# Rows of the attention by batch, input weights fetched by one transfer, the first group solved in 30 steps, a planner that counts instruction blocks

## The chip, the cores and the metric

The kernel runs on one core of one Trainium2 chip. The metric is the device time of one execution in microseconds. A core has five engines with a queue each: TensorE (PE in the profile; PEld is its weight loads), VectorE (DVE), ScalarE (ACT), GpSimd (POOL) and SyncE (SP), which here only issues transfers. A queue runs in the order in which the program was written. The engines wait for each other through semaphores.

## What is computed

A delta-rule attention (4 batches, 8 heads, 768 tokens, head size 48), then two MLPs with hidden size 2048, each with its own weights:

```python
for t in range(S):                                   # attention
    y[:, :, t] = einsum('bhd,bhde->bhe', q[:, :, t], state)
    v_old = einsum('bhde,bhd->bhe', state, kt)       # kt: normalised key
    state = state + bt * einsum('bhd,bhe->bhde', kt, vt - v_old)
...
h = x @ w_in; g = P(h) / (Q(h) + 1e-6); x = g @ w_out   # first MLP, P cubic, Q quadratic in |h|
...
h = x @ w_in; g = h * tanh(softplus(h)); out = g @ w_out # second MLP
```

The inputs are float64 in memory; the weights are 8-byte numbers that the kernel turns into pairs of 4-byte ones.

## The kernel before

**Attention.** The 768 tokens are cut into 24 steps of 32 tokens (`C`), four steps to a group (`GU`), six groups. The four 32-row quarters of the partitions hold eight of the 32 batch-head pairs each. For a group, `norms` normalises the keys, `prepare` transposes keys and queries and multiplies them (`gram`, L407), `inverse` solves a unit triangular system for the whole group, and `finish` transposes the solution (L499) and multiplies it by beta (L504). Then `step` runs four times, one after the other, since each needs the state of the one before: `ks` (L575: keys times state), `rest` (L581: v minus that, on DVE), `uu` (L587: solution times rest), `s_mm` (L601: the new state), `y_mm` (L622: the output, a part from the state and a part from U), `x_mm` (L634, L638: transposes the output into the MLP's layout). For the first step the state is a tile of zeros.

**The solve.** Groups in `HALVED` (0 and 1) solve two 16-row halves side by side, in 14 steps of two instructions each (L468, L474), and join the halves by two products on PE, `right` (L519) and `left` (L526), of 128 small matmuls each, with an ACT and a DVE operation behind. Other groups take 30 steps and no product. Group 0 is solved on DVE, the others on POOL.

**Rows.** Before, the batch-head pairs lie in the partitions such that the head dimension in `x` comes out permuted. That is why the first MLP's `w_in` is fetched in seven transfers for each 128-column slice (L705, L708, L709), why its slabs are read in the order `slab`, and why `x_mm` has two transposes and four small products.

**Weights.** `Weights.plan` converts a slice of 128 columns of `w_in` or rows of `w_out` (a half): fetch into one of five raw buffers, clamp on POOL (L712, one of three work buffers), fold on ACT (L717), shift and tail on DVE (L726, L731), high part on ACT (L738), low part by two matmuls on PE (L746, L747) and an ACT copy (L750), and a store to memory. 24 halves are planned ahead of the first MLP's first unit.

**MLPs.** A group of 512 tokens is a stretch of 16 units per MLP. A unit is `up` (L846, nine matmuls), the elementwise chain on ACT, DVE and POOL, and `down` (L852, nine matmuls). The first stretch is the first MLP on group 0, the second is the second MLP on group 0 with the four steps of group 1 between its units, and so on.

**Order.** `Plan` holds every operation with an engine, a duration the author wrote down, what it reads and writes, and a due time. `order` lists them by a simulated clock: of the operations that are ready on an engine it takes the one that is due earliest, less its `early`. `run` then writes the program in that order, and fills planned gaps of PE ahead of the MLPs with up to six matmuls that nobody reads (`heat`, L994).

## Time and profile before

| | us |
|---|---|
| runs (3): median, lowest, highest | 1161.53, 1159.25, 1161.65 |
| the profiled execution, its own time | 1155.55 |
| span in its trace | 1153.8 |
| busy: PE, PEld | 1061.0, 850.6 |
| busy: DVE, ACT, POOL | 672.4, 604.0, 543.2 |
| first matmul of the first MLP starts | 125.91 |
| first matmul of the second MLP starts, about | 229 |

PE is busy in 92% of the span. Busy time is an average over stretches with different limits: ahead of 125.9 us no MLP work runs, behind 327 us PE is nearly always busy. The granted clock of PE is 0.97 on the mean and lower in parts of the first 130 us.

### The profile page before, as it was taken

Reading aid. Unit: us, or ns where it says so; the run is one execution under the profiler, and the core shown is the slowest. Engines: PE = TensorE matmul, PEld = TensorE weight load, DVE = VectorE, ACT = ScalarE, POOL = GpSimd, SP = SyncE. Lnnn points to the kernel's source line nnn. Section 1 sums busy time; section 2 is a strip of 40 time slices with the busy share of each in tenths; the row PEclk is TensorE's granted clock in tenths of the full one; section 3 lists DMA queues with packets and bytes.
Section 4 is the critical chain, followed back from the end, with each engine's and each line's share of the span. In section 5 each row is a group of like instructions: output and inputs, shape, how many; then the busy total and the mean of one; then the engine's idle time right before and its main releaser. Section 6 shows DMA issues by size and latency. Waiting matters only on the chain.

```text
span 1153.8 us, 34301 instructions
## 1 busy us (share of the span) xinstructions
PE 1061.0 (92%) x14560; PEld 850.6 (74%) x14560; DVE 672.4 (58%) x1017; ACT 604.0 (52%) x1065; POOL 543.2 (47%) x697
## 2 busy tenths in 40 slices
PE   5477898879999989999999998999999999999997
PEld 4355676667777767777877776877777778889997
DVE  6744687786769934239952239952347668831211
ACT  3333786654568742248842248842257568742221
POOL 4101388754537797818628217728226357600000
PEclk8868998989999999999999999999999999999999
DMA  5755752387776746366765366865466456766773
GB/s 151 211 169 196 237 159 70 112 286 249 238 251 158 233 124 184 109 160 162 223 190 172 113 159 162 224 196 166 113 168 172 131 144 189 191 181 188 202 206 82
DMA packets 118200, 202.86 MB, mean 176 GB/s; under 512 B 48128, under 2 KB 61440, under 8 KB 118048
## 3 DMA queue, kind: packets, MB, share of 16 engines
q1 hardware_dynamic: 117072, 199.41, 60.2%
q8 instruction: 114, 1.87, 0.7%
q10 hardware_dynamic: 848, 1.18, 0.4%
q14 instruction: 38, 0.31, 0.1%
q0 software_dynamic: 128, 0.10, 0.0%
HBM read 168.40 MB, written 29.88 MB: 172 GB/s over the span
## 4 chain that ended last, share of the span: by engine, by line
PE 60%; DVE 5%; ACT 5%; POOL 4%; DMA 3%; issue 2%; SPq 1%; DVEq 0%; POOLq 0%; ACTq 0%
PE b_h L846 25%; PE b_o L852 19%; PE b_o L861 4%; PE b_t L622 3%; PE b_t L601 2%; PE b_t L587 1%; PE b_t L861 1%; POOL xs L474 1%; POOL tmp L468 1%; PE b_t L575 1%; DMA wd<-win 1%; DMA arena<-in_q_dram 1%; POOL mq L884 1%; DVE mq L889 1%; DVE b_r L890 1%
## 5 line engine op out<-in xcount | busy, mean ns | idle before, releaser
L846 PE MATMUL b_h<-x,win 128*128 128x512 f32 x1620 | 411.8, 400 | 16.9 <-DVE ms L886 8.1
L846 PEld LDWEIGHTS b_h<-x,win 128*128 128x128 f32 x1620 | 299.6, 189 | 88.6 <-DVE ms L886 14.1
L852 PE MATMUL b_o<-gh,wout 128*128 128x512 f32 x1332 | 336.7, 398 | 7.0 <-POOL gh L893 5.7
L852 PEld LDWEIGHTS b_o<-gh,wout 128*128 128x128 f32 x1332 | 246.0, 189 | 63.4 <-POOL gh L893 10.3
L884 POOL TENSOR_TENSOR mq<-mq,mr 128x512 f32<-128x512 f32 x96 | 124.2, 1294 | 108.2 <-ACT mr L882 104.8
L897 DVE TENSOR_TENSOR gh<-mq,gh 128x512 fp32r<-128x512 f32 x96 | 72.5, 755 | 163.0 <-ACT mq L896 162.8
L895 ACT ACTIVATE gh<-b_h 128x512 fp32r<-128x512 f32 x96 | 57.3, 597 | 205.3 <-PE b_h L846 201.4
L893 POOL TENSOR_TENSOR gh<-mq,gh 128x512 fp32r<-128x512 f32 x96 | 124.1, 1293 | 56.3 <-ACT gh L892 55.4
L885 DVE TENSOR_TENSOR ms<-ms,b_h 128x512 f32<-128x512 f32 x96 | 65.6, 683 | 53.9 <-ACT ms L883 53.2
L712 POOL TENSOR_SCALAR arena<-arena 128x384 f32<-128x384 f32 x64 | 34.8, 546 | 97.9 <-PE b_h L746 55.8
L876 ACT ACTIVATE mr<-mq,cst 128x512 f32<-128x512 f32 x96 | 69.0, 720 | 20.4 <-POOL mq L884 19.5
L878 ACT ACTIVATE mq<-b_h 128x512 f32<-128x512 f32 x96 | 56.8, 591 | 42.9 <-PE b_h L846 37.7
L889 DVE SCALAR_TENSOR_TENSOR mq<-mq,b_r 128x512 f32<-128x512 f32 x96 | 65.1, 679 | 22.7 <-ACT b_r L888 22.3
L883 ACT ACTIVATE ms<-b_h,ab 128x512 f32<-128x512 f32 x96 | 73.8, 770 | 4.1 <-PE b_h L846 3.7
L468 POOL TENSOR_TENSOR tmp<-xs 128x58 f32<-128x58 f32 (+9 forms) x134 | 70.1, 523 | 9.7
L886 DVE SCALAR_TENSOR_TENSOR ms<-ms,ab,b_h 128x512 f32<-128x512 f32 x96 | 71.7, 747 | 2.9
L474 POOL TENSOR_TENSOR xs<-xs,tmp 128x58 f32<-128x58 f32 (+9 forms) x134 | 68.3, 510 | 10.5
L890 DVE SCALAR_TENSOR_TENSOR b_r<-ms,ab,b_r 128x512 f32<-128x512 f32 x96 | 72.0, 750 | 0.0
L892 ACT CAST gh<-mq 128x512 fp32r<-128x512 f32 x96 | 59.0, 614 | 21.9 <-DVE mq L891 20.1
L891 DVE SCALAR_TENSOR_TENSOR mq<-mq,b_r 128x512 f32<-128x512 f32 x96 | 65.8, 686 | 2.8
L888 ACT ACTIVATE b_r<-mr 128x512 f32<-128x512 f32 x96 | 57.7, 601 | 6.5 <-DVE mq L891 5.7
L896 ACT ACTIVATE mq<-b_h 128x512 f32<-128x512 f32 x96 | 56.9, 593 | 0.0
(179 smaller groups left out, 1415.0 us busy)
## 6 DMA issues: line engine op xcount, KB each, us to landing
win<-wd SPq DMA_DIRECT2D x164, 384.0 KB
wout<-wd SPq DMA_DIRECT2D x164, 384.0 KB
arena<-in_moe_w_out_dram SPq DMA_DIRECT2D x32, 384.0 KB
wd<-x SPq DMA_DIRECT2D x24, 384.0 KB
wd<-win SPq DMA_DIRECT2D x16, 384.0 KB
wd<-wout SPq DMA_DIRECT2D x16, 384.0 KB
arena<-in_moe_w_in_dram SPq DMA_DIRECT2D x16, 384.0 KB
arena<-in_moe_w_in_dram SPq DMA_DIRECT2D x32, 96.0 KB
```

The costliest lines, as they stand in the source:

```text
L468: eng.tensor_tensor(out=tv, in0=part(row, slice(j, j + 1), slice(j + 1, L)).to_broadcast([128, nb, j, n]), in1=part(xs, slice(0, j), slice ...
L474: eng.tensor_tensor(out=to, in0=to, in1=tv, op=ALU.add)
L846: nc.tensor.matmul(out=h, lhsT=win[:, a, j], rhs=x[:, c, slab[j]], start=n == 0, stop=n == 8)
L852: nc.tensor.matmul(out=self.banks[f"o{d}"], lhsT=wout[:, a, d], rhs=gh[:, c], start=first and j == 0, stop=last and j == 2,)
L876: act(out=r, in_=q, func=ACTF.Ln, bias=k["c"])
L883: p.add("ACT", 775, lambda: act(out=s, in_=h, func=ACTF.Identity, scale=k["a3"], bias=k["a2"]), [hb], [sb])
L884: p.add("POOL", 1335, lambda: P.tensor_tensor(out=q, in0=q, in1=r, op=ALU.mult), [rb], [qb])
L886: p.add("DVE", 750, lambda: V.scalar_tensor_tensor(out=s, in0=s, scalar=k["a1"], in1=h, op0=ALU.add, op1=ALU.mult), [hb], [sb])
L889: p.add("DVE", 685, lambda: V.scalar_tensor_tensor(out=q, in0=q, scalar=1.0 + 1e-6, in1=rp, op0=ALU.add, op1=ALU.mult), ["r"], [qb])
L890: p.add("DVE", 750, lambda: V.scalar_tensor_tensor(out=rp, in0=s, scalar=k["a0"], in1=rp, op0=ALU.add, op1=ALU.mult), [sb], ["r"])
L893: p.add("POOL", 1320, lambda: P.tensor_tensor(out=gh[:, 1], in0=q, in1=gh[:, 0].bitcast(F32), op=ALU.subtract), [qb], [ghb])
L897: p.add("DVE", 755, lambda: V.tensor_tensor(out=gh[:, 1], in0=q, in1=gh[:, 0].bitcast(F32), op=ALU.subtract), [qb], [ghb])
```

## The change

It does six things.

1. A quarter of the partitions now holds the eight heads of one batch (`batch`), so that `x` comes out in the order of the model dimension. k and q are fetched in two transfers instead of four, v in four instead of two; `w_in` of the first MLP is fetched in one transfer per slice; `slab` goes; `x_mm` is three transposes.
2. Group 0 leaves `HALVED`: its solve takes 30 steps on DVE and no joining products.
3. The first step of all drops its work on the zero state: no `ks`, no `rest`, half of `y_mm`. The state tiles are no longer cleared.
4. `betas`: fetch and transpose of beta are planned operations; they stood in `setup`.
5. The planner gives PE operations a count of instructions (`ins`) and lets PE wait at every 256 of them until `FETCH` ns after the block before; planned transfers are taken first come, first served.
6. Constants: `NEAR` halved; group 0's queries get `early=FIRST`; the operation on `ab` loses its `early`.

```diff
-HALVED = (0, 1)
+HALVED = (1,)
-NEAR = 40000
+NEAR = 20000
+FETCH = 4000
+AHEAD_INS = 384
...
+        word, block, landed = -AHEAD_INS, 0, []
...
+                ins = self.ops[i][7]
+                word += ins
+                while ins and word >= 256:
+                    word -= 256
+                    part = min(word, ins) * self.ops[i][1] // ins
+                    block = max(end - part, block + FETCH)
+                    end = block + part
...
+    @staticmethod
+    def batch(e):
+        return 2 * (e % 2) + 1 - e // 2
...
         def x_mm():
-            for a in range(2):
-                out = x_ps.rearrange("p k (a n) -> p a k n", a=2)[:, a, 0:2]
-                nc.tensor.transpose(out=out, in_=y[:, a * 4 * D:a * 4 * D + 128], identity=self.ident)
-            for a in range(2):
-                for r in range(2):
-                    rows = slice(64 * r, 64 * r + 64)
-                    nc.tensor.matmul(
-                        out=x_ps[rows, 2, 64 * a:64 * a + 64], lhsT=y[rows, a * 4 * D + 128:(a + 1) * 4 * D],
-                        rhs=self.ident[rows, rows], start=True, stop=True,
-                    )
+            for k in range(3):
+                nc.tensor.transpose(out=x_ps[:, k], in_=y[:, k * 128:(k + 1) * 128], identity=self.ident)
...
-        p.add("PE", 780, ks, [kb, f"{sb}0", f"{sb}1"], [bc], early=lead(AHEAD, G))
-        p.add("DVE", 560, rest, [bc, vb], ["r2"], early=lead(AHEAD, G))
-        p.add("PE", 760, uu, ["r2", f"xt{g}"], [bc], early=lead(AHEAD, G))
+        if u:
+            p.add("PE", 780, ks, [kb, f"{sb}0", f"{sb}1"], [bc], early=lead(AHEAD, G), ins=128)
+            p.add("DVE", 560, rest, [bc, vb], ["r2"], early=lead(AHEAD, G))
+        p.add("PE", 760, uu, ["r2" if u else vb, f"xt{g}"], [bc], early=lead(AHEAD, G), ins=128)
...
-            elif self.n:
+            else:
                 nc.sync.dma_start(out=raw, in_=self.w_in.rearrange("(k p) f -> p k f", p=128)[:, :, cols])
-            else:
-                w = self.w_in.rearrange("(m r d) f -> m d r f", r=2, d=48)
...
-        slab = (1, 0, 2) if m == 1 else (0, 1, 2)
```

What it moves shows in the order of the queues. On PE, from the last work ahead of the solve's result to the first step. Before (L519 and L526 are the joining products, L994 the filler, L746 and L747 the low part of a weight half, L407 a `gram` of the queries, L575 `ks`, L587 `uu`):

```order
L994 MATMUL b_o_100<-ident_138 128x128 x6
L519 MATMUL b_t_102<-xt_162,lg_160 32x16 x128
L994 MATMUL b_o_100<-ident_138 128x128 x2
L746 MATMUL b_h_99<-arena,ident_138 128x384
L747 MATMUL b_h_99<-x_112,minus 128x384
L526 MATMUL b_t_102<-xs_161 16x16 x128
...
L407 MATMUL b_t_103<-kq_146 32x32 x32
L575 MATMUL b_t_102<-su_156,kq_145 32x48 x32
...
L587 MATMUL b_t_102<-r_159,xt_162 32x48 x32
```

And now, in the same place (L447 is `gram`, L1016 the filler, L627 `uu`, L641 `s_mm`):

```order
L447 MATMUL b_t_103<-kq_145 32x32 x32
...
L447 MATMUL b_t_103<-kq_146 32x32 x32
...
L447 MATMUL b_t_103<-kq_147 32x32 x32
L1016 MATMUL b_o_100<-ident_138 128x128 x6
L447 MATMUL b_t_103<-kq_148 32x32 x32
L1016 MATMUL b_o_100<-ident_138 128x128 x6
L627 MATMUL b_t_102<-qv_143,xt_162 32x48 x32
L1016 MATMUL b_o_100<-ident_138 128x128 x2
L641 MATMUL b_o<-u_158,kn_142 64x48
```

All four `gram` of group 0's queries now stand ahead of the first `uu`; before, one stood ahead of it and two behind, between the steps. Both joining products and the first `ks` are gone.

On DVE, where the transposition of v (L245, now L279) cuts into the solve. Before:

```order
L468 TENSOR_TENSOR tmp_163<-xs_161,b_o 128x72
L474 TENSOR_TENSOR b_o<-b_o,tmp_163 128x2x3x12
L245 STREAM_TRANSPOSE qv_143<-ev_134 128x48x8x4
L468 TENSOR_TENSOR tmp_163<-xs_161,b_o 128x88
L474 TENSOR_TENSOR b_o<-b_o,tmp_163 128x2x4x11
```

And now (L508 and L514 are the two instructions of a step, L453 the masking of a `gram`):

```order
L508 TENSOR_TENSOR tmp_163<-xs_161,b_o 128x168
L514 TENSOR_TENSOR b_o<-b_o,tmp_163 128x7x24
L453 TENSOR_TENSOR am_151<-b_t_103,mask_140 128x256
L279 STREAM_TRANSPOSE qv_143<-ev_134 128x48x8x4
L508 TENSOR_TENSOR tmp_163<-xs_161,b_o 128x184
```

It stood behind step 3 of 14 and stands behind step 7 of 30. In neither does a weight conversion stand between the solve's first and last step.

On ACT, at the start of the second MLP. Before (L895 and L896 are the second MLP's function, L717 the fold and L738 the high part of a weight half):

```order
L738 CAST wout_120<-arena 128x384
L895 ACT_TABLE_LOAD
L895 ACTIVATE gh_131<-b_h_99 128x512
L717 ACT_TABLE_LOAD
L717 ACTIVATE arena<-arena 128x384 x2
L895 ACT_TABLE_LOAD
L895 ACTIVATE gh_130<-b_h_98 128x512
L896 ACTIVATE mq_122<-b_h_98 128x512
```

And now (L917 and L918 are that function, L762 the high part):

```order
L762 CAST wout_121<-arena 128x384
L917 ACT_TABLE_LOAD
L917 ACTIVATE gh_130<-b_h_98 128x512
L918 ACTIVATE mq_122<-b_h_98 128x512
L917 ACTIVATE gh_131<-b_h_99 128x512
L918 ACTIVATE mq_122<-b_h_99 128x512
```

The two folds stand ahead of the first table load now, and two table loads are gone.

## Rows read from the trace of the kernel before

**Rows 1.** The page: busy time, share of the span and instructions of each engine.

```profile
PE 1061.0 (92%) x14560; PEld 850.6 (74%) x14560; DVE 672.4 (58%) x1017; ACT 604.0 (52%) x1065; POOL 543.2 (47%) x697
```

**Rows 2.** Stretches: length, busy time of PE, PEld, DVE, ACT, POOL, clock, DMA.

```profile
78.20:125.90 47.70, 38.06 (x1423) 29.24 (x1423) 21.33 (x40) 22.42 (x52) 8.00 (x11) 0.89 0.57 185
125.90:229.00 103.10, 90.67 (x1164) 69.77 (x1162) 81.61 (x124) 74.08 (x133) 77.63 (x101) 0.95 0.45 139
229.00:327.00 98.00, 91.09 (x1537) 70.67 (x1538) 72.43 (x121) 53.10 (x107) 49.13 (x60) 0.97 0.79 258
327.00:1154.00 827.00, 798.91 (x9353) 648.07 (x9351) 448.89 (x645) 427.42 (x721) 390.98 (x478) 1.00 0.62 170
```

**Rows 3.** Timeline of PE, 57 to 126 us: start, length, [idle before and releaser].

```profile
57.23 2.47 PE L519 MATMUL b_t<-xt,lg 32*32 32x16 f32 x169 [12.29 <-DVE xt L499]
62.41 1.37 PE L519 MATMUL b_t<-xt,lg 32*32 32x16 f32 x87 [2.71 <-issue]
...
78.18 0.68 PE L587 MATMUL b_t<-r,xt 32*32 32x48 f32 x26
...
125.91 1.32 PE L846 MATMUL b_h<-x,win 128*128 128x512 f32 x5
```

**Rows 4.** DMA queues, 78.2 to 125.9 us: packets, MB, share.

```profile
q8 instruction: 11, 0.18, 1.6%
```

**Rows 5.** Waits, 78.2 to 125.9 us: us in total, times, longest.

```profile
POOL arena L712 <- PE b_h L746: 30.7, 7, 7.0
...
PE b_t L587 <- issue: 4.3, 3, 2.2
...
PE b_o L622 <- issue: 4.0, 3, 2.0
```

**Rows 6.** Timeline of DVE: the solve of group 0 and what follows.

```profile
35.95 2.00 DVE L448 STREAM_TRANSPOSE b_o<-lg 128x1024 f32<-128x1024 f32 x1
...
41.19 0.18 DVE L468 TENSOR_TENSOR tmp<-xs,b_o 128x28 f32<-128x28 f32 x1 [0.22 <-ACT xs L485]
...
41.64 0.21 DVE L468 TENSOR_TENSOR tmp<-xs,b_o 128x52 f32<-128x52 f32 x1
...
46.34 2.80 DVE L245 STREAM_TRANSPOSE qv<-ev 128x1536 f32<-128x1536 f32 x1 [3.70 <-DMA ev<-in_v_dram]
...
50.78 0.27 DVE L468 TENSOR_TENSOR tmp<-xs,b_o 128x112 f32<-128x112 f32 x1
...
51.40 0.27 DVE L468 TENSOR_TENSOR tmp<-xs,b_o 128x112 f32<-128x112 f32 x1
...
55.28 1.89 DVE L499 STREAM_TRANSPOSE xt<-b_o 128x1024 f32<-128x1024 f32 x1
...
72.38 0.42 DVE L504 TENSOR_TENSOR xt<-xt,beta_t 128x256 f32<-128x256 f32 x1
```

**Rows 7.** Timelines of ACT and, last row, PE at the start of the second MLP.

```profile
237.83 1.28 ACT L717 ACT_TABLE_LOAD   x1
239.13 0.94 ACT L717 ACTIVATE arena<-arena 128x384 f32<-128x384 f32 x2
240.08 1.28 ACT L895 ACT_TABLE_LOAD   x1
...
242.51 2.07 PE L846 MATMUL b_h<-x,win 128*128 128x512 f32 x4 [5.33 <-ACT mq L896]
```

**Rows 8.** Timeline of PE: one `x_mm` of group 1, then four transposes of a `prepare`.

```profile
286.66 0.44 PE L634 MATMUL b_t<-ident,y 128*128 128x128 f32 x2
...
287.40 1.43 PE L846 MATMUL b_h<-x,win 128*128 128x512 f32 x5
...
321.07 0.60 PE L395 MATMUL b_t<-ident,kn 128*128 128x128 f32 x4
321.43 2.32 PE L846 MATMUL b_h<-x,win 128*128 128x512 f32 x9
```

**Rows 9.** Groups by line, 57 to 126 us: busy us, mean ns of one.

```profile
L731 DVE SCALAR_TENSOR_TENSOR arena<-arena,b_r 128x384 int32<-128x384 int32 x15 | 8.3, 551 | 0.4
```

More of the change, by code (lines that the diff above doesn't have):

```diff
@@ L85, in order @@
         for i in range(n - 1, -1, -1):
-            engine, ns, fn, need, more, due, early = self.ops[i]
+            engine, ns, fn, need, more, due, early, ins = self.ops[i]
             if due is not None:
@@ L108, in order @@
             queue = ready[engine]
-            pick = min((x for x in queue if x[0] <= t), key=lambda x: (late[x[1]], x[1]))
+            pick = min((x for x in queue if x[0] <= t), key=lambda x: (x[0] if engine == "DMA" else late[x[1]], x[1]))
             queue.remove(pick)
@@ L116, in order @@
                 was = wide
+                ins = self.ops[i][7]
[5 more added lines that the diff above has]
+                    end = block + part
+            if engine == "DMA":
+                landed.append(end + self.LANDING)
             free[engine] = end
@@ L138, in run, with lead @@
                 fn()
-def lead(ns, G):
+FIRST = 20000
+def lead(ns, G, what=""):
+    if G == 0 and what == "q":
+        return FIRST
     return ns if G > 1 else NEAR * G
@@ L547, in finish @@
         for g in range(GU):
-            p.add(engine, 690 if engine == "POOL" else 420, scale(g), (), [f"xt{g}"], early=lead(AHEADX, G))
+            p.add(engine, 690 if engine == "POOL" else 420, scale(g), ["beta"], [f"xt{g}"], early=lead(AHEADX, G))
     def step(self, p, u):
@@ L616, in y_mm @@
         def y_mm():
-            for part in range(2):
+            for part in range(u == 0, 2):
                 for m in range(M):
@@ L624, in y_mm @@
                             rhs=U[rows, m, :] if part else S[rows, c, m, :],
-                            start=not part and m == 0, stop=part > 0 and m == M - 1, skip_group_check=True,
+                            start=part == (u == 0) and m == 0, stop=part > 0 and m == M - 1, skip_group_check=True,
                         )
```

137 lines of the change are left out of this document (70 added, 67 removed).

## The prediction

> **What bounds the kernel now.** The page's busy shares come first: PE 92% [rows 1]. An average hides where the other 8% lie, so the stretches come next [rows 2]. From 327 us to the end PE is busy 798.9 of 827 us: there only PE work counts. From 125.9 to 229 (first MLP, group 0) it is 90.7 of 103.1, from 229 to 327 91.1 of 98. Ahead of 125.9 no MLP runs; the attention's first group, a chain of single operations, decides when the MLPs start. So the questions are: how much earlier does the first MLP matmul (125.91 us, last of [rows 3]) come, is that kept, and what PE work goes in the rest.
>
> In the last part ahead of it, 78.2 to 125.9, PE runs the four steps of group 0, from the first `uu` (78.18) on. It is busy 38.06 of 47.7 us and idle 9.6. The waits name who ends that idle time: "issue", where no engine and no transfer is late, 4.3 us before `uu` and 4.0 before `y_mm` [rows 5], and little else on PE. The same happens inside one loop of like matmuls: L519 stops 2.71 us after 169 of its 256, with nothing to wait for [rows 3]. The DMA rows say what is missing: 11 packets of 16 KB for the instruction queue in 47.7 us [rows 4]. The order of the program has 2,844 PE instructions there (a float32 matmul is two loads and two matmuls in the trace, a transpose one of each), so a packet is 256 instructions, 47.7/11 = 4.3 us apart. Small matmuls use up 256 instructions faster than that. So this part is bound by PE's instruction supply, with PE's own work close behind.
>
> **The change, part by part.** *Start of the solve.* Before, the matrix is turned at 35.95 to 37.95, and the first of the 14 steps starts at 41.19, after an ACT copy [rows 6]. Ahead of it the change takes six of seven issues per `w_in` slice off SP. That is SP time, not path, but ACT and DVE get weights earlier and may reach the copy earlier. Ends: 38.4 (turn plus copy) and 41.2; I take 40.
>
> *The solve itself.* A step's pace: 41.64 − 41.19 = 0.45 us at 28 elements, 51.40 − 50.78 = 0.62 at 112 [rows 6], so 0.45 + 0.0020 per element above 28. The 14 steps have 1,120 elements in all: 6.3 + 1.5 = 7.8 us. The 30 steps have j(31−j), 4,960 in all: 13.5 + 8.3 = 21.8 us. That is 14 us more on DVE, in the path. Elements beyond 112 are not in the trace; a straight line is assumed, since two pieces of it agree with the instruction's length (0.18 at 28, 0.27 at 112).
>
> *In between.* The turn of v takes 2.80, and DVE waited 3.70 for v's transfer [rows 6]; with the solve longer and the transfer issued from a shorter SP queue I take 0.5 of that wait (ends 0 and 3.7). Three maskings stand between the steps now, 0.42 each as the 0.42 us operations of the same size (1.3 in all).
>
> *Behind the solve.* Before: turn of the solution at 55.28, two products with PE starved (2.71 us in the first), and beta at 72.38, so that `uu` started at 78.18 after `ks` and `rest` on zeros. Now: the turn 1.9, beta 0.4, `uu`. Sum: 40 + 21.8 + 2.8 + 0.5 + 1.3 + 1.9 + 0.4 + 0.2 for a hop = 69 us (ends 67 and 74), against 78.2.
>
> *The four steps.* From `uu` to the first `up` the new order has 2,408 instructions: two `gram` less, half a `y_mm` less, four `x_mm` at 6 for 20, two weight halves more. At 4.3 us per 256 that is 40.4 us. But PE pauses during the solve, and after the pause of 12.29 us at 57.23 it ran 169 matmuls with their loads, some 340 instructions, before it starved [rows 3]: 5.7 us' worth lie ready. That leaves 34.7. PE's own work is 38.06 less some 5 for what is gone, plus 2 for the two halves: 35. Two limits this close do not overlap fully, and the pause lowers the clock (0.89 on the mean in this part, [rows 2]). I take 38; ends 35 and, if nothing is gained, 47.7. First `up` at 69 + 38 = 107 instead of 125.9: **−18.9 us** (ends −4 and −24).
>
> *Is it kept?* The stretch behind it is the same work in nearly the same order, and PE is busy 88% of it [rows 2]; I cost the shift of it at nothing. What covers this is that the weight halves keep up. POOL waited 30.7 us for a buffer that PE's low part had to free [rows 5], so the conversion was waiting for PE, not PE for it, and PE gets to it sooner now. DVE has 21.3 us of work in the 47.7 [rows 2]; with two more halves at 2 x 0.55 [rows 9] and the turn of group 1's queries, as long as v's, it is some 26 of the new 38: 70%, no bound.
>
> *Start of the second MLP.* ACT loads its function tables three times, with two folds between; PE stands for 5.33 us behind it [rows 7]. In the new order the folds stand ahead and two loads go: 2 x 1.28 + 0.94 = **−3.5 us** (ends 0, if a fold ahead is late instead, and −5.3).
>
> *`x_mm`.* Its slot on PE before is 287.40 − 286.66 = 0.74 us; four transposes take 321.43 − 321.07 = 0.36 [rows 8]; three take no more. 0.38 for each of the 20 steps of groups 1 to 5, where PE is the bound: **−7.6 us** (−5 if PE waits in some of them anyway).
>
> *At nothing*: beta's planned fetch (POOL is free then), the uncleared state, v's four issues for two (SP has more time than before), `ab` without `early`.
>
> Sum: −18.9 − 3.5 − 7.6 = −30.0. Against the profiled execution's own 1155.55 us that is 1125.5. It is 6.0 below the median of the runs, so I put the median at 1161.5 − 30.0 = **1131.5**. The ends of the parts give −9 to −37: 1152 to 1124.
>
> **A rule against it.** The trace shows PE stopping in the middle of like matmuls for 2.71 us, and packets 4.3 us apart [rows 3, 4]. The Trainium skill (Runtime: NRT & Kernel Launch, Instruction fetch mechanics) says that instructions come in blocks of 256 while the current ones run, and that the cost of crossing a block is mostly hidden. By that rule the idle time would have another cause and stay. The blocks agree with the trace; "mostly hidden" doesn't, where the matmuls are small.
>
> **The rivals.**
> - *The idle time isn't the supply.* The 9.6 us stay, and only PE's own work goes: from `uu` to `up` 35 + 9.6 = 44.6, first `up` at 113.6, −12.3 − 3.5 − 7.6 = −23.4: 1138. For it: only three loops show it plainly. Against: 11 packets fit the 2,844 instructions.
> - *The gain is given back in the second stretch.* Group 1's steps now stand later among its units: its last `x_mm` behind the 32nd `up`, where it was behind the 30th. If group 1's own chain (POOL's solve, v) sets the pace, the first MLP on group 1 starts some 8 us earlier at most. With `x_mm` in groups 2 to 5 (16 x 0.38 = 6.1) that gives −14: 1147. For it: POOL is busy 77.6 of 103 us [rows 2]. Against: PE is busy 91 of 98 in the second stretch and waits for POOL little.
> - *Slower: the conversion becomes the bound.* Between the first and last step of the solve DVE converts no weights, and 13 of 24 halves remain behind it. If they go through one after another, at clamp, fold, shift, tail, high and low part and copy, six operations of some 0.55 us like that in [rows 9] and 1 to 2 for PE, 5 us a half, plus a wait for a fetch into one of five buffers, 6 in all, it is 13 x 6 = 78 us: first `up` at 147, +21 − 11 = +10: 1171. It decides above 5.4 us a half ((139 − 69)/13); before, 11 went through in 47.7 us, 4.3 each, and they waited for PE.
>
> **How the numbers follow.** Forecast 1131.5: 0.63. Idle time stays: 0.14. Given back: 0.15. Slower: 0.05; its turning point, within 0.2% (2.3 us, about what a measurement can tell): 0.03. Faster 0.92. The range takes in the ends of the parts and the second rival: 1121 to 1151.
>
> **What would show it.** In the new trace: the first `uu` near 69 and the first `up` near 107, 9 or 10 instruction packets between them, hardly any "issue" before the first step. The solve's 60 DVE instructions in about 22 us without, and 27 with, v's turn and the maskings. One table load at the start of the second MLP, and no 5 us gap on PE there. `x_mm` as three transposes in a slot below 0.4. The second MLP's start about 20 us earlier than 229, the first MLP on group 1 about 23 earlier than 327. It is wrong if DVE's pace rises above the line beyond 112 elements, if `up` waits for weights, or if the two later starts have moved by less than the first.

## The result and the profile after

The changed kernel takes 1120.1 us (median of four runs, 1118.1 to 1122.2), the kernel before 1160.4 beside it: a ratio of 0.965 (0.963 to 0.968). The forecast of 1131.5 is 11 us above that, and the range ended at 1121. One execution of `more_ins` (1462 us) and one of the kernel before beside it (2564 us) were slow ones and are left out of the medians below. The profiled execution of the changed kernel took 1122.17 us, with a span of 1120.5; before it was 1155.55 and 1153.8. So the profiles lie 33.4 us apart and the medians 40.3.

The page of the kernel after, busy time and instructions of each engine (of before: [rows 1]):

```profile
PE 1044.5 (93%) x13788; PEld 844.6 (75%) x13788; DVE 684.3 (61%) x1045; ACT 601.4 (54%) x1062; POOL 544.2 (49%) x695
```

PE is busy 16.5 us less, so half of the 33 us in the profiles is PE work that is gone and half is idle time. Where they went shows in stretches of the kernel after: from the start to the first `uu`, to the first `up`, the first stretch (16 units), the first four units of the second MLP, on to unit 64, and the rest. Columns as in [rows 2].

```profile
0.00:66.31 66.31, 38.33 (x675) 32.30 (x675) 53.99 (x110) 24.20 (x48) 16.63 (x45) 0.81 0.66 195
66.31:113.10 46.79, 36.91 (x1205) 27.77 (x1205) 28.31 (x47) 24.19 (x56) 8.65 (x12) 0.84 0.66 213
113.10:214.30 101.20, 90.43 (x1162) 70.99 (x1160) 81.53 (x127) 77.77 (x137) 81.86 (x107) 0.93 0.50 161
214.30:231.30 17.00, 14.77 (x65) 11.23 (x55) 16.35 (x25) 11.33 (x24) 13.34 (x15) 0.90 0.89 316
231.30:486.60 255.30, 245.21 (x3889) 194.08 (x3889) 164.03 (x245) 130.58 (x237) 155.66 (x219) 0.99 0.67 193
486.60:1120.50 633.90, 618.82 (x6807) 508.21 (x6805) 340.09 (x494) 333.32 (x564) 268.08 (x299) 1.00 0.62 173
```

The first number behind a stretch is its length, the next PE's busy time. The same stretches of the kernel before, of a second profiled execution of the changed kernel (`same_again`, below) and of the run with part 1 of the change alone (`rows_only`, below), beside the terms of the forecast:

| stretch | before | after | again | part 1 alone | after − before | forecast |
|---|---|---|---|---|---|---|
| to the first `uu` | 78.2 | 66.3 | 67.1 | 70.5 | −11.9 | −9.2 |
| to the first `up` | 47.7 | 46.8 | 44.8 | 47.7 | −0.9 | −9.7 |
| units 0 to 16 | 103.0 | 101.2 | 101.2 | 102.9 | −1.8 | 0 |
| units 16 to 20 | 23.4 | 17.0 | 16.9 | 24.0 | −6.4 | −3.5 |
| units 20 to 64 | 258.5 | 255.3 | 256.0 | 254.9 | −3.2 | −3.0 |
| unit 64 to the end | 643.0 | 633.9 | 634.4 | 635.4 | −9.1 | −4.6 |
| sum | 1153.8 | 1120.5 | 1120.4 | 1135.4 | −33.3 | −30.0 |

(The 7.6 us for 20 `x_mm` are split 8 to 12.) The sum was only 3.3 us off, but its terms were not that near: one was nearly empty, and the others were larger than forecast. That they cancelled is luck.

The largest miss first. PE from the first `uu` on, timeline of the kernel after (start, length, idle before and releaser):

```profile
66.31 1.50 PE L627 MATMUL b_t<-qv,xt 32*32 32x48 f32 x64 [6.01 <-DVE xt L544]
...
82.66 0.53 PE L662 MATMUL b_o<-su,kq 64*32 64x48 f32 x27 [1.97 <-issue]
...
87.89 0.54 PE L615 MATMUL b_t<-su,kq 64*32 64x48 f32 x31 [2.37 <-issue]
...
99.97 0.37 PE L627 MATMUL b_t<-r,xt 32*32 32x48 f32 x14
104.30 1.32 PE L627 MATMUL b_t<-r,xt 32*32 32x48 f32 x50 [3.96 <-issue]
```

The first `uu` came at 66.3, near the 69 forecast. Then PE still stops in the middle of like matmuls, as in [rows 3], once for 3.96 us. The waits of PE from 66.3 to 113.1 (us in total, times, longest) and the instruction queue in the same time (packets, MB, share), which answer to [rows 4, 5]:

```profile
PE b_t L627 <- issue: 4.8, 2, 4.0
PE b_o L662 <- issue: 2.7, 2, 2.0
PE b_t L615 <- issue: 2.4, 1, 2.4
```

```profile
q8 instruction: 9, 0.15, 1.3%
```

There are 9 packets, as forecast, but 5.2 us apart where 11 packets lay 4.3 apart before. PE is busy 36.9 us (forecast: 35) and idle 9.9, as long as before (9.6); three other executions of this prologue (below) have 35.2 to 38.5 busy and 6.6 to 9.4 idle.

What PE stands for shows when its instructions in the trace are counted, loads and matmuls. The first stop of over 0.25 us comes after 625 of them, at 75.4 us, and the later ones 255 or 510 after the one before (a few records are missing). At each, PE goes on 1.3 to 1.6 us after a 16 KB packet of the instruction queue has landed. Cut into such blocks of 256, the stretch has eight whole ones: three with much work of PE's own (4.45, 5.79 and 4.93 us) and no stop behind them, and five with less (2.85 to 4.40 us) and stops of 0.7 to 4.0 us.

The solve of group 0 on DVE, which answers to [rows 6]:

```profile
35.68 1.98 DVE L488 STREAM_TRANSPOSE b_o<-lg 128x1024 f32<-128x1024 f32 x1
...
42.95 2.93 DVE L279 STREAM_TRANSPOSE qv<-ev 128x1536 f32<-128x1536 f32 x1
...
51.62 0.41 DVE L508 TENSOR_TENSOR tmp<-xs,b_o 128x240 f32<-128x240 f32 x1
...
52.51 0.40 DVE L508 TENSOR_TENSOR tmp<-xs,b_o 128x240 f32<-128x240 f32 x1
...
63.91 1.89 DVE L539 STREAM_TRANSPOSE xt<-b_o 128x1024 f32<-128x1024 f32 x1
65.83 0.43 DVE L544 TENSOR_TENSOR xt<-xt,beta_t 128x256 f32<-128x256 f32 x1
```

A step of 240 elements takes 52.51 − 51.62 = 0.89 us; the straight line of the forecast gives 0.45 + 0.0020 x 212 = 0.87. The turn of v has no wait in front.

The start of the second MLP on ACT, which answers to [rows 7], has one table load, and PE (last row, its own timeline) waited 2.1 us for the `mq` that starts at 220.82, instead of 5.33:

```profile
219.03 1.28 ACT L917 ACT_TABLE_LOAD   x1
220.32 0.60 ACT L917 ACTIVATE gh<-b_h 128x512 fp32r<-128x512 f32 x1
220.82 0.59 ACT L918 ACTIVATE mq<-b_h 128x512 f32<-128x512 f32 x1
...
221.46 3.91 PE L868 MATMUL b_h<-x,win 128*128 128x512 f32 x9 [2.13 <-ACT mq L918]
```

An `x_mm` on PE, timeline, against 0.74 us before ([rows 8]): the slot is 605.50 − 605.20 = 0.30.

```profile
605.20 0.55 PE L673 MATMUL b_t<-ident,y 128*128 128x128 f32 x3
605.50 1.17 PE L874 MATMUL b_o<-gh,wout 128*128 128x512 f32 x4
```

### The profile page after: what moved, and what is told of

The parts are those of the page before. It is cut to its first block, busy times and chain, and to the rows that moved or that the text cites. A ratio compares the mean times of both kernels' runs of the same rounds, so it can differ in the third digit from the quotient of the medians.

```text
span 1120.5 us, 32550 instructions
## 1 busy us (share of the span) xinstructions
PE 1044.5 (93%) x13788; PEld 844.6 (75%) x13788; DVE 684.3 (61%) x1045; ACT 601.4 (54%) x1062; POOL 544.2 (49%) x695
## 4 chain that ended last, share of the span: by engine, by line
PE 71%; DVE 10%; POOL 5%; ACT 4%; DMA 4%; issue 4%; SPq 0%; DVEq 0%; POOLq 0%; ACTq 0%
PE b_h L868 28%; PE b_o L874 22%; PE b_o L883 4%; PE b_t L662 3%; DMA arena<-in_moe_w_in_dram 2%; PE b_t L627 2%; PE b_t L641 2%; PE b_h L770 2%; PE b_t L883 1%; POOL xs L514 1%; PE b_t L447 1%; PE b_t L615 1%; POOL tmp L508 1%; PE b_t L435 1%; DVE qv L279 1%
## 5 line engine op out<-in xcount | busy, mean ns | idle before, releaser
L917 ACT ACTIVATE gh<-b_h 128x512 fp32r<-128x512 f32 x96 | 57.3, 597 | 208.5 <-PE b_h L868 204.8
L911 DVE SCALAR_TENSOR_TENSOR mq<-mq,b_r 128x512 f32<-128x512 f32 x96 | 65.5, 682 | 29.7 <-ACT b_r L910 27.2
L514 POOL TENSOR_TENSOR xs<-xs,tmp 128x58 f32<-128x58 f32 (+9 forms) x134 | 69.9, 522 | 10.5
L508 POOL TENSOR_TENSOR tmp<-xs 128x58 f32<-128x58 f32 (+9 forms) x134 | 68.7, 513 | 9.9
L914 ACT CAST gh<-mq 128x512 fp32r<-128x512 f32 x96 | 58.9, 613 | 17.4 <-DVE mq L913 16.9
L918 ACT ACTIVATE mq<-b_h 128x512 f32<-128x512 f32 x96 | 56.9, 593 | 0.0
## 6 DMA issues: line engine op xcount, KB each, us to landing
kns<-kn SPq DMA_DIRECT2D x12, 256.0 KB
```

The source lines that it names most:

```text
L508: eng.tensor_tensor(out=tv, in0=part(row, slice(j, j + 1), slice(j + 1, L)).to_broadcast([128, nb, j, n]), in1=part(xs, slice(0, j), slice ...
L514: eng.tensor_tensor(out=to, in0=to, in1=tv, op=ALU.add)
```

## The experiments

All kernels in one table: the median, the same less the median of the kernel before on the same chip, the ratio's interval, and from the profile the start of the first `up`, of unit 16 (the second MLP), of unit 64, and the span. Runs of one kernel spread by 1 to 10 us, so medians tell differences of some 3 us and the stages of a profile less.

| kernel | median | − before | ratio | first `up` | unit 16 | unit 64 | span |
|---|---|---|---|---|---|---|---|
| before | | | | 125.9 | 228.9 | 510.8 | 1153.8 |
| after | 1120.1 | −40.3 | 0.963–0.968 | 113.1 | 214.3 | 486.6 | 1120.5 |
| same_again | 1119.3 | −39.6 | 0.963–0.970 | 111.9 | 213.1 | 486.0 | 1120.4 |
| rows_only | 1140.2 | −19.2 | 0.980–0.989 | 118.2 | 221.1 | 500.0 | 1135.4 |
| join0 | 1123.6 | −35.9 | 0.964–0.974 | 110.2 | 212.4 | 485.6 | 1120.4 |
| zero_step | 1138.1 | −20.8 | 0.978–0.988 | 120.9 | 224.5 | 505.2 | 1143.0 |
| zero_kept | 1121.5 | −35.4 | 0.968–0.972 | 112.1 | 212.2 | 484.4 | 1118.0 |
| no_blocks | 1130.2 | −29.2 | 0.971–0.980 | 106.8 | 216.0 | 495.5 | 1131.5 |
| blocks_late | 1129.1 | −29.8 | 0.971–0.977 | 108.7 | 215.1 | 491.7 | 1126.4 |
| f5000 | 1127.0 | −30.5 | 0.971–0.977 | 110.2 | 214.2 | 490.8 | 1125.1 |
| old_leads | 1132.6 | −26.9 | 0.974–0.982 | 114.9 | 218.4 | 493.8 | 1131.8 |
| near_only | 1131.5 | −25.4 | 0.974–0.981 | 110.8 | 219.8 | 492.6 | 1131.4 |
| near10000 | 1141.8 | −17.1 | 0.981–0.989 | 111.3 | 217.1 | 502.6 | 1140.6 |
| first_only | 1132.2 | −24.7 | 0.975–0.983 | 117.4 | 226.7 | 502.3 | 1136.6 |
| more_ins | 1125.4 | −31.5 | 0.969–0.977 | 117.2 | 216.7 | 489.3 | 1123.6 |
| more_ins9 | 1133.7 | −23.9 | 0.977–0.984 | 125.8 | 225.7 | 497.1 | 1130.0 |
| more_time | 1127.2 | −29.7 | 0.970–0.977 | 117.0 | 217.8 | 490.9 | 1125.7 |
| xmm_old | 1132.5 | −25.0 | 0.975–0.982 | 109.0 | 209.3 | 486.8 | 1126.9 |
| two_tables | 1121.5 | −36.0 | 0.967–0.972 | 110.6 | 209.9 | 485.2 | 1120.1 |
| loads_inside | 1123.2 | −33.6 | 0.969–0.974 | 110.5 | 211.1 | 486.8 | 1121.8 |

Up to the first `up`, `same_again`, `two_tables` and `loads_inside` are the changed kernel itself: with it, four executions, 110.5 to 113.1, mean 111.5. Against that mean the prologues below are read.

### The same kernel again

> The changed kernel, once more, beside the kernel before: it tells how far one profiled execution lies from the median of its runs. The profiled pair differed by 33.4 us, the medians by 40.3. If the forecast failed at the profile's own sum, the medians differ by some 40 again and this profile is far below the first one's span of 1120.5. If the two profiled executions lay on opposite sides of their medians (5.9 below, 2.0 above): medians 33 to 40 apart, and stage by stage this profile repeats the first within 1 to 3 us (first up 111 to 115).

The second profile repeats the first: the same span, and no stretch of the table above further off than 2.0 us. The medians are 39.6 apart. The 38 runs of the kernel before beside all these kernels have a median of 1158.0, from 1152.2 to 1163.8. Its profiled 1155.55 is 2.4 below that median, and the two profiled executions of the changed kernel, 1122.2 both times, are 2.3 above the median of its eight runs, 1119.8. So the best difference of medians is 1158.0 − 1119.8 = 38.2, and 4.7 of the 4.9 us by which it exceeds the profiles' 33.3 come from the choice of the profiled executions.

### Part 1 alone, and what is left of it in the order as changed

`rows_only` is the kernel before with these edits, all queues ordered as before:

```diff
-            for a in range(2):
-                out = x_ps.rearrange("p k (a n) -> p a k n", a=2)[:, a, 0:2]
...
+            for k in range(3):
+                nc.tensor.transpose(out=x_ps[:, k], in_=y[:, k * 128:(k + 1) * 128], identity=self.ident)
...
-                w = self.w_in.rearrange("(m r d) f -> m d r f", r=2, d=48)
...
+                nc.sync.dma_start(out=raw, in_=self.w_in.rearrange("(k p) f -> p k f", p=128)[:, :, cols])
```

> The kernel before with part 1 of the change alone: rows by batch, fewer transfers for k, q, v and w_in, x_mm as three transposes, no slab; the order of the queues stays that of the kernel before. By the prediction's terms: 20 x 0.38 us of x_mm behind the first stretch (-7.6) and some 1 to 4 us in the prologue, where four x_mm have 56 instructions less, one packet more or less is saved, and six issues per slice leave SP: -8 to -12, 1148 to 1152. If SP's issues and late weights were what held the prologue back: -13 or more in the prologue alone, 1140. If x_mm's slot is filled by other waits: -2, 1158.

It gains 19.2 us, about half of the whole: the time of the second theory (1140), but not its place. Its profile has 7.6 us ahead of the first `uu`, where that theory wanted 13 or more, and 10.6 behind unit 16. DVE in the prologue of `rows_only`:

```profile
38.43 0.18 DVE L476 TENSOR_TENSOR tmp<-xs,b_o 128x28 f32<-128x28 f32 x1
...
39.81 2.93 DVE L255 STREAM_TRANSPOSE qv<-ev 128x1536 f32<-128x1536 f32 x1
```

The solve starts at 38.4, not 41.2, and v is there: the wait of 3.70 us [rows 6] is gone. The forecast had these two in its way to the first `uu`, smaller (1.2 and 3.2 us) and as it says from the shorter SP queue, which is part 1.

```diff
         def x_mm():
-            for k in range(3):
-                nc.tensor.transpose(out=x_ps[:, k], in_=y[:, k * 128:(k + 1) * 128], identity=self.ident)
+            for a in range(2):
+                out = x_ps.rearrange("p k (a n) -> p a k n", a=2)[:, a, 0:2]
...
```

> The changed kernel with x_mm in its old form in all 24 steps (two transposes and four products of 64 rows), the order of the queues unchanged; the head dimension lands permuted in x, so what the MLPs compute is not the reference's. By the prediction's 0.38 us a step: +7.6 behind the first stretch, 1128. By what part 1 alone gained behind the first stretch (10.7 us over 20 steps, 0.53 each): +10.7, 1131. If the rest of part 1 (SP's issues, the slab) made up that gain: +4 or less, 1124.

From unit 16 to the end `xmm_old` takes 1126.9 − 209.3 = 917.6 us, the changed kernel 906.2 and 907.3: 10.3 to 11.4 for 20 steps, 0.51 to 0.57 each. Timeline of PE, the old form in the new order:

```profile
605.45 0.44 PE L674 MATMUL b_t<-ident,y 128*128 128x128 f32 x2
605.82 0.45 PE L678 MATMUL b_t<-ident,y 64*64 64x64 f32 x8
606.20 0.50 PE L882 MATMUL b_o<-gh,wout 128*128 128x512 f32 x1
```

The slot is 0.75 against 0.30, so 0.45 of it is PE's own; over all 20 steps the mean slots are 0.738 before and 0.288 after, 9.0 us in all. The remaining 1 to 2 us are no more than executions of one order differ by: from unit 16 on, `more_ins`, `more_ins9`, `more_time` and `zero_kept`, whose edits lie ahead of it, take 904.3 to 907.9.

### Parts 2 and 3: joining products and the first step

```diff
-HALVED = (1,)
+HALVED = (0, 1)
```

> The changed kernel with one part undone: group 0 is solved in 14 steps again and its halves are joined by the two products on PE (1,024 more PE instructions, four packets' worth), everything else as changed. If PE's instruction supply sets the pace from the products on, the solve is 14 us shorter on DVE, and the way from the turned solution to beta is some 15 us longer (57.2 to 72.4 in the trace of the kernel before): the first up moves by +1 to +3 us, and the time too (1121 to 1123). If the supply is not the limit and the products cost only PE's own work (2 x some 3.5 us and two hops), the first up is some 5 us earlier than in the changed kernel (108) and the time 1115.

First `uu` at 67.4 (0.3 to 1.9 later than in the four executions with the change), first `up` at 110.2 (1.3 earlier than the mean), unit 64 at 485.6, and the same span: leaving the products out gained nothing that the profile shows, though the planner made another order for this kernel too. The median, 3.4 us higher, has an interval that overlaps that of the changed kernel. `rows_only`, with the products and an order as before, has its first `uu` 3.2 us later: a `gram`, `ks` and the products of a weight half stand on PE between the joining products and `uu` there (64.5 to 70.5), here those of a weight half alone (65.5 to 67.4).

```diff
-        if u:
-            p.add("PE", 780, ks, [kb, f"{sb}0", f"{sb}1"], [bc], early=lead(AHEAD, G), ins=128)
+        p.add("PE", 780, ks, [kb, f"{sb}0", f"{sb}1"], [bc], early=lead(AHEAD, G), ins=128)
...
```

> The changed kernel with part 3 undone: the first step reads the zero state again (ks, rest and the state's half of y_mm: 256 more PE instructions, one packet), and the state tiles are cleared. By what the two lengthened steps showed (a packet of extra instructions cost its PE work, 2.1 us, and hardly more): first uu 1 to 2 us later for ks and rest ahead of it, first up 3 to 4 us later. By the prediction's 4.3 us a packet: 5 to 6 later. Of this the end keeps between nothing (as with the joining products) and all of it: 1120 to 1124.

18 us, far more than any theory had. But the planner also ordered the program anew. The same work inside the planned `uu` and `y_mm`, with the order kept:

```diff
         def uu():
+            if not u:
+                ks()
+                rest()
...
-            for part in range(u == 0, 2):
+            for part in range(2):
```

> The changed kernel with the first step reading the zero state again (ks and rest inside the planned uu, the state's half inside the planned y_mm, state tiles cleared), the order of all else as changed. If the 18 us of the planned version are the work itself: 1135 or more. If they are mostly the order: one packet at 2.3 to 3.3 us (what the lengthened steps showed) and ks, rest and two hops ahead of the first uu, some 1.5 us: first up 4 to 5 us later than the two runs of the changed kernel (111.9 and 113.1), 116 to 118, and the time 1122 to 1125.

First `uu` at 67.0, first `up` at 112.1, and a span 2.4 below that of the changed kernel; the median is 1.3 to 2.2 above its medians. The work on the zero state costs next to nothing: `ks` runs while PE waits for the solve, and the 128 instructions more behind the first `uu` found time in PE's standing (45.1 us from `uu` to `up`). So the 18 us of `zero_step` are its order.

### Parts 5 and 6: the order

The next seven kernels change only numbers and rules of the planner, and with them the order:

```diff
-FETCH = 4000
+FETCH = 0
```

> The changed kernel with the planner's waits for instruction blocks taken out, so that only the order of the program differs: the steps of group 1 stand earlier among the units of the second stretch again, its last x_mm ahead of the 32nd up. If the gain behind 300 us (the first MLP on group 1, -8.5 us) came from that order, it is lost here: 1126 to 1129. If it came from elsewhere (the change of rows, weights that arrive earlier), the time stays at 1120 within 2 us. The first up stays at 113 within 2 us by both.

The first `up` is the earliest of all, at 106.8, with 4.4 us of idle PE in the four steps instead of 9.9, and the kernel is 10 us slower. It loses them twice. In units 0 to 16, PE waits for the turned solution of group 1 ahead of its first joining product (view of PE's waits, 146.8 to 216 us):

```profile
PE b_t L559 <- DVE xt L539: 9.0, 1, 9.0
```

And the second MLP's start has the order of the kernel before again: ACT, timeline.

```profile
223.94 1.28 ACT L917 ACT_TABLE_LOAD   x1
225.24 0.60 ACT L917 ACTIVATE gh<-b_h 128x512 fp32r<-128x512 f32 x1
225.85 1.28 ACT L741 ACT_TABLE_LOAD   x1
227.15 0.52 ACT L741 ACTIVATE arena<-arena 128x384 f32<-128x384 f32 x1
227.69 1.28 ACT L917 ACT_TABLE_LOAD   x1
228.98 0.60 ACT L917 ACTIVATE gh<-b_h 128x512 fp32r<-128x512 f32 x1
229.48 1.08 ACT L918 ACTIVATE mq<-b_h 128x512 f32<-128x512 f32 x2
```

Both `mq` come behind a fold and two more loads; PE waits 7.2 us for them, and units 16 to 20 take 25.1 us instead of 17.0.

```diff
...
+                mlp = mlp or wide
...
-                    block = max(end - part, block + FETCH)
+                    block = max(end - part, block + (FETCH if mlp else 0))
```

> The changed kernel, with the planner's waits for instruction blocks only from the first MLP's first unit on: the prologue is ordered as without them (first up at 106.8 there, 6.3 us earlier than in the changed kernel, at 4.4 us of idle PE instead of 9.9), the second stretch with them. If the waits earn their gain in the second stretch and cost 6 us in the prologue: first up 107, time 1114. If an earlier first up is eaten up before the second MLP starts, as with the joining products: first up 107, time 1118 to 1121. Three table loads at the start of the second MLP would add 4 to 5.

One table load there now, but the wait for group 1's solution is back:

```profile
PE b_t L560 <- DVE xt L540: 8.9, 1, 8.9
```

The first `up` is 2.8 us earlier than the changed kernel's mean, and the end 5.9 later. The median, 1129.1, is above both theories.

```diff
-FETCH = 4000
+FETCH = 5000
```

> The changed kernel with the planner's constant for a packet at 5000 ns instead of 4000 (the packets of the four steps came 5.2 us apart). A try at a faster kernel: if the constant's truth is what counts, 1115 to 1119. All other changes of the order so far (five of them) cost 9 to 22 us, by waits of PE for POOL or DVE in units 8 to 16 or by later steps of group 2; if this is another such order: 1128 to 1135.

No gain: 7 us slower; its profile loses 7.6 us between units 32 and 48, where PE waits 6.6 us for a copy on ACT ahead of a `gram`:

```profile
PE b_t L447 <- ACT kq L439: 6.6, 1, 6.6
```

```diff
-NEAR = 20000
+NEAR = 40000
...
-    if G == 0 and what == "q":
-        return FIRST
...
-    plan.add("ACT", 230, lambda: nc.scalar.activation(out=ab[:, 4:6], in_=ab[:, 4:6], func=ACTF.Abs), (), ["ab"])
+    plan.add("ACT", 230, lambda: nc.scalar.activation(out=ab[:, 4:6], in_=ab[:, 4:6], func=ACTF.Abs), (), ["ab"], early=20000)
```

All three together (`old_leads`), the first alone (`near_only`), the second alone (`first_only`):

> The changed kernel with the three lead times of the plan as before (part 6 of the change): NEAR doubled, group 0's queries without their own lead, ab with its lead. I cost these at nothing in the prediction. If that holds: 1120 within 2.3 us, first up at 113. If the position of the queries' gram ahead of the first uu is worth the instructions that it keeps out of the four steps (two gram of 64 PE instructions with their loads, half a packet, 2.2 us, and a hop to POOL and DVE), the first up is 2 to 4 us later and the time 1122 to 1124.

> The changed kernel with the lead of group 1 doubled back to that of the kernel before (NEAR), the other two lead times as changed. The three together cost 12 us. If this lead carries that cost (group 1's operations push into the first stretch: units 4 to 8 took 24.2 us instead of 17.4 with all three undone): 1128 to 1133. If it is the queries' lead of group 0: 1120 within 2.3 us.

> The changed kernel with the lead of group 0's queries alone undone (their gram stand later, some between the four steps). If this lead carries the 12 us of the three: 1128 to 1133, first up at 115, and PE waits some 25 us for beta's products behind the solve as with all three undone. If it is group 1's lead: 1120 within 2.3 us.

12, 11 and 12 us by their medians (13 to 15 against the kernel before on the same chip); the lead of `ab` was not undone alone. The costs don't add, so it isn't the single constant that carries a price. Each order loses in its own places. `near_only` starts the first `up` 2.3 us earlier than the first profile of the changed kernel and takes 109.0 us for units 0 to 16 instead of 101.2; of PE's waits there (149.9 to 219.8 us) the first is POOL, which is solving group 1 and gets to `gh` late:

```profile
PE b_o L874 <- POOL gh L915: 7.7, 3, 5.2
```

```diff
-NEAR = 20000
+NEAR = 10000
```

> The changed kernel with group 1's lead halved once more. Going back to twice the lead cost 11 us. If that is so because group 1's operations push ahead of the first stretch's units: units 0 to 16 take less than 101 us and the time is 1115 to 1118. If the lead is needed for group 1's chain now (its last step stands at the 32nd up instead of just ahead of it): the start of the first MLP on group 1 waits, 1123 to 1128.

Units 0 to 16 took 105.8 us, units 28 to 32 35.6 instead of 29.0 and units 64 to 80 85.3 instead of 80.2: 22 us. That the lead is needed fits the second theory in units 28 to 32, at a price above its own; the losses elsewhere it did not have.

### What a packet of instructions costs in the four steps

```diff
-            for m in range(M):
+            for m in [m for _ in range(5 if u == 2 else 1) for m in range(M)]:
```

> The changed kernel with the uu of the third step of every group... of group 0 and all later groups (u == 2 is only in group 0) written five times over: 512 more PE instructions, two packets' worth, some 3.5 us of PE work if nothing is late (26 matmul records take 0.68 us); the result is the same. If the instruction supply sets the pace of the four steps (a packet every 4.3 us before, 5.2 after): first up 8.6 to 10.4 us later than in the changed kernel, 122 to 123.5. If the idle time is something else and PE's own work counts: 3.5 us later, 116.6. How much of it reaches the end is open: the gain of the first up of the run with the joining products (-2.9) was gone by the 28th up, so I expect half of it, 1124 to 1126; all of it would be 1130.

> The changed kernel with the third step's uu written nine times over: 1,024 more PE instructions, four packets' worth, some 8.6 us of PE work by what the five-fold one added (36.9 to 41.2 us busy for two packets); same result. If a packet costs what PE does with it and a little standing: first up 8.6 to 10 us later, 122 to 123. If each packet costs 4.3 us in such a run of like matmuls (the prediction's rule; five-fold +4.1 then owed to a stall that fell away): 17 later, 130.

(`more_ins9` has 9 for 5.) Against the mean of 111.5 the first `up` is 5.7 us later with two more packets and 14.2 with four, both between the two theories. The first two cost 2.8 each, the next two 4.3. Within the long run of like matmuls, PE's timeline in `more_ins9` shows the pace (128 of these records are 64 float32 matmuls and, with the loads, 256 instructions):

```profile
90.20 1.56 PE L627 MATMUL b_t<-r,xt 32*32 32x48 f32 x128 [0.54 <-issue]
94.20 1.99 PE L627 MATMUL b_t<-r,xt 32*32 32x48 f32 x128 [2.44 <-issue]
98.20 2.78 PE L627 MATMUL b_t<-r,xt 32*32 32x48 f32 x128 [2.02 <-issue]
101.66 2.29 PE L627 MATMUL b_t<-r,xt 32*32 32x48 f32 x101 [0.67 <-issue]
```

Every 256 instructions PE stops, and the blocks start 3.5 to 4.0 us apart, whether PE works 1.56 or 2.78 us in one (the granted clock is 1.00 in the first of these blocks, 2.4 GHz, and 0.50 in the third, 1.2 GHz). So the idle time is the supply, and the pace of packets does bind where all matmuls are small. Within such a block PE's work hides behind the packet: the stop shrinks from 2.44 to 0.67 us as the work grows.

```diff
+            for _ in range(8 if u == 2 else 0):
+                nc.tensor.matmul(
+                    out=self.banks["h0"][:, 0:384], lhsT=self.ident,
+                    rhs=self.xs.rearrange("p a b -> p (a b)")[:, 0:384], start=True, stop=True,
+                )
```

> The changed kernel with eight more 128x384 float32 matmuls behind the third step's uu, into a bank that nobody reads then: 32 more PE instructions (an eighth of a packet), some 3.6 us of PE work. Supply theory: PE stands for packets there, and the work falls into that idle time or keeps the next packet's fetch covered: first up 0 to 2 us later, 113 to 115. Work theory: the full 3.6 us, 116.7. If work and supply do not overlap (a packet is asked for only when PE enters the one before, so that time spent in a packet counts in full once it exceeds the fetch of some 4.4 us): between 2 and 3.6.

First `up` at 117.0, 5.5 later than the mean and above the 116.7 of the work theory. The stretch from `uu` to `up`, columns as in [rows 2], of this kernel and of `no_blocks`:

```profile
65.90:117.00 51.10, 41.17 (x1220) 29.78 (x1221) 29.12 (x48) 24.16 (x56) 8.67 (x12) 0.89 0.59 196
```

```profile
65.80:106.80 41.00, 36.65 (x1205) 27.87 (x1206) 21.98 (x43) 22.91 (x53) 8.09 (x11) 0.80 0.61 199
```

Work that needs an eighth of a packet counted in full: PE is busy 41.2 us instead of 35.2 to 38.5 and stands 9.9 instead of 6.6 to 9.9. But the eight matmuls stand in a block of 256 instructions that has no stop in the changed kernel either (87.89 to 93.47 there, 86.95 to 97.43 here), so there was no idle time for them to fill. This run doesn't show that work and supply never overlap. `more_ins9` shows that within a block they do, and `no_blocks` runs as many instructions with as much work (36.7 us) and stands 4.4 us. What these traces show is a limit that changes from block to block: a short block waits for its packet, a long one is PE's own work, and the sum of both lies above either total.

### The second MLP's start

```diff
-            p.add("ACT", 2000 if first and G < 5 else 600, lambda: act(out=gh[:, 0], in_=h, func=ACTF.Mish), [hb], [ghb] + (["table"] if first and G < 5 else []))
+            def mish():
+                if f == 1 and G == 0:
+                    A.preload_act_table_set("natural_log_exp_and_others")
+                act(out=gh[:, 0], in_=h, func=ACTF.Mish)
+
+            p.add("ACT", 2000 if first and G < 5 else 600, mish, [hb], [ghb] + (["table"] if first and G < 5 else []))
```

> The changed kernel with two more table loads on ACT at the start of the second MLP (2 x 1.28 us, between the function of its first and of its second unit), the order of all other work unchanged. If the two loads are the gain there: PE's wait for the second MLP's function grows from 2.1 to some 4.7 us, units 16 to 20 take 19.5 instead of 17.0, and the time is 1122.5. If other work covers the loads: 1120. If the delay goes on into group 1's steps: 1124 or more.

Two more loads, and PE's wait is 2.1 us as without them:

```profile
PE b_h L868 <- ACT mq L923: 2.1, 1, 2.1
```

Units 16 to 20 took 15.4 us, and units 16 to 32 93.4, as in the changed kernel (93.0 and 93.4). In `loads_inside` the same two stand one operation earlier, ahead of the first unit's `mq`:

```diff
-            p.add("ACT", 595, lambda: act(out=q, in_=h, func=ACTF.Mish), [hb, "table"], [qb])
+            def mish2():
+                if first and G == 0:
+                    A.preload_act_table_set("natural_log_exp_and_others")
+                act(out=q, in_=h, func=ACTF.Mish)
+
+            p.add("ACT", 595, mish2, [hb, "table"], [qb])
```

> The changed kernel with two table loads (2.56 us) put between gh and mq of the second MLP's first unit on ACT, the order of all else as changed. If the place counts (PE's third unit needs the bank that this mq frees): PE's wait of 2.1 us there grows to some 4.7, units 16 to 20 take 2.6 us more than in the changed kernel, and the time is 1122 to 1123. If loads cost nothing there either: wait of 2.1, 1120, and the 5 to 7 us of the other orders come from something else than ACT.

Its ACT, timeline:

```profile
218.56 0.60 ACT L917 ACTIVATE gh<-b_h 128x512 fp32r<-128x512 f32 x1
219.17 1.28 ACT L920 ACT_TABLE_LOAD   x1
220.46 1.28 ACT L921 ACT_TABLE_LOAD   x1
221.75 0.60 ACT L921 ACTIVATE mq<-b_h 128x512 f32<-128x512 f32 x1
```

PE's wait there:

```profile
PE b_h L868 <- ACT mq L921: 4.8, 1, 4.8
```

It grows from 2.1 to 4.8 us, by the two loads (2.57), units 16 to 20 take 21.1 and units 16 to 32 96.5. So not the number of loads counts but what stands ahead of the `mq` that frees the bank for the third unit's `up`.

## Why the prediction was wrong where it was

**Base.** It was made against one profiled execution of before and carried to the median of three runs. Both lay off: 2.4 below and 3.5 above the median of 38 runs (1158.0). Of the 11.7 us between 1131.5 and the 1119.8 of eight runs, 3.5 are this base, 3.3 the sum (33.3 for 30.0), and 4.9 that the two profiled executions lay nearer together than the medians.

**The sum: near by luck.** The four steps gave 8.8 us less than forecast. The way to the first `uu` gave 2.7 more, units 0 to 16 1.8, the start of the second MLP 2.9 and the stretch from unit 20 to the end 4.7. So the step that failed below made the forecast too fast; what carried the time below the range is the base, the choice of the profiled executions, and these terms that were too small.

**Start and solve: right mechanism, a little early.** First `uu` 66.3 and 67.1 (65.5 and 66.0 in `two_tables` and `loads_inside`), forecast 69, range 67 to 74. The solve began at 38.5 (forecast 40) and took 25.4 us with v's turn and the maskings (26.4); the pace by element held up to 240 elements. But what was gained there came mostly from part 1 (7.6 us in `rows_only`), little of it from the missing products (`join0`: 0.3 to 1.9).

**The four steps: the failed term.** The step was: supply 34.7, PE's own work 35, "two limits this close do not overlap fully", 38. Measured 46.8 and 44.8 (45.1 and 44.6 in `two_tables` and `loads_inside`): 35.2 to 38.5 of PE's own work and 6.6 to 9.9 of stops. Two things were wrong in it. It took the larger of two totals and 3 us on top, where the limit changes from block to block of 256 instructions: the stops behind short blocks come on top of the time of the long ones. And 4.3 us a packet, 47.7/11, is no pace of the supply, since PE's own work is in it: the packets came 5.2 us apart here on the mean and two of them 7.7, and the blocks of the long run of like matmuls 3.5 to 4.0. The credit of some 340 instructions that "lie ready" does show: PE ran 625 to its first stop, 369 more than the one packet brought that had come into use by then. The rival "the idle time isn't the supply" had the right time for the first `up` (113.6) for the wrong reason: the stops are at the supply, as the 256-instruction pattern above shows, but PE's work hides only those of the long blocks. The Trainium skill (Runtime: NRT & Kernel Launch, Instruction fetch mechanics) has blocks of 256, which the pattern agrees with, and their crossing "mostly hidden", which the stretches of small matmuls here do not agree with (stops of 0.7 to 4.0 us behind five of eight blocks).

**"Is it kept": half right.** Units 0 to 16 took as long as before within 2 us, so the shift was kept there. The second MLP started 14.6 us earlier and the first MLP on group 1 18.3, both more than the first `up` (12.8), so the rival "given back" falls. What the prediction did not see is that this holds for this order. In the nine other orders, units 0 to 16 were 1.0 us (`join0`) to 8.1 us longer, and a first `up` that came 2.8 and 4.7 us earlier (`blocks_late`, `no_blocks`) was lost there in a new wait.

**Second MLP's start: right place, too small.** Forecast −3.5, measured −6.4. Part 1 alone has 24.0 us there and all three loads, so the gain is the order's. Two loads ahead of the `mq` explain 2.7 us of it, by `loads_inside`; the folds that stood there with them and the waits for `x` of up to 1 us that are gone are the likely rest, which was not tried.

**`x_mm`: right mechanism, size off.** 0.36 was the time of four transposes, an upper bound for three, and it was used as the value. The slot is 0.29: 0.45 saved, not 0.38; with what else goes with it 0.51 to 0.57.

**"At nothing": wrong for the constants.** The leads and the block count were costed at nothing by themselves. `NEAR`, `FIRST` and the block count, undone one by one, cost 10 to 12 us, through the order. Part 1 gives 19 of the 40 us. In the profiles the step from `rows_only` to the changed kernel is 14.9 us: 4.2 to the first `uu`, 7.0 in units 16 to 20 and 3.7 elsewhere; in the medians it is 20.1, of which 4.8 come from the choice of the profiled executions (2.8 below its median for `rows_only`, 2.0 above for the changed kernel). This half goes with the order that the remaining edits make together; the runs cannot share them out among these edits, since each edit undone makes another order, and no run had the order of after with the rows of before.

**Slower: the conversion.** It did not come up: PE waits for no weight between `uu` and `up`.

**Open.** What asks for an instruction packet, and why one came 7.7 us behind the last (94.18 and 101.84 us by the packets' own times in the trace), when PE had stood since 100.3.

## What to carry to other kernels

Where PE runs many small matmuls, go through its instructions 256 at a time: here a block with some 3 us of work of its own was mostly followed by a stop, of up to 4 us, and one with 5 us by none. The larger of the two totals is too little. A change that alters the planner's numbers is a change of order: compare the order at every place where PE waits for another engine, and hold the order fixed (put the work inside an existing operation) to learn what the work itself costs. An earlier start is worth what the next chain leaves of it: of nine other orders, the one with the earliest first `up` ended 11 us late.

## What the runs showed of the hardware

Two table loads back to back on ACT took 2.57 us, and the function behind them started 0.01 us later. The Trainium skill (ScalarE: Activation LUTs, What ACT_TABLE_LOAD costs) gives 1283 ns for a load, as here, and 1380 ns more for a drain, by which two would take 5.3; no drain shows in these rows.

In a run of like small matmuls (`more_ins9`) PE stops every 256 instructions and the blocks start 3.5 to 4.0 us apart, also where its own work in a block is 1.6 us. In the traces of before, after, `same_again`, `rows_only`, `more_ins` and `more_ins9`, PE goes on 1.2 to 1.6 us after a packet of the instruction queue has landed, at every stop of over 0.25 us between the solve of group 0 and the first `up`.
